# Attention and a gated MLP on one core: scores and P times V by half tiles of queries, with the last scores in the bank of P times V

## The chip, the cores and the metric

One NeuronCore of a Trainium2 chip runs the whole program in one launch. The metric is device microseconds of one execution. The core has a matrix engine (TensorE, PE in the profile, with PEld for its weight loads), three other compute engines (VectorE or DVE, ScalarE or ACT, GpSimd or POOL), and SyncE (SP), which issues the transfers. All of them run their own queue of instructions in order and wait for each other by semaphores. TensorE writes to PSUM, which the kernel uses in banks of 128 partitions by 512 words of 4 bytes; DVE and ACT read it from there.

## The reference

```python
# 8 batches, 8 heads, 576 positions, 64 columns per head
scores = q @ k.T / sqrt(64) + bias            # bias = -slope[h] * |i - j|
mask   = (i - j >= 0) & (i - j < 128)         # a query sees itself and the 127 keys before it
attn   = softmax(where(mask, scores, -1e9))
x      = (attn @ v), heads side by side       # 8 x 576 x 512
h      = relu(x @ w_in)                       # 512 x 1024
u, v   = h[..., :512], h[..., 512:]
v_n    = (v - mean) / sqrt(var + 1e-6)        # over the 512 columns
v_s    = w_spatial @ v_n + b_spatial          # over the 576 positions
out    = (u * v_s) @ w_out                    # 512 x 512
```

All of it is float32. A query of tile t (128 queries, five tiles, the last of 64) needs keys of tiles t-1 and t alone; a half tile of 64 queries needs just 192 keys, its own 64 and the 128 before them.

## The kernel before, in words

The work is 32 pairs of heads, four to a batch, and behind each batch its gated MLP. The first five pairs (batch 0, and the first of batch 1) go another way (`raw_tile`, L418), which the change leaves as it is but for names. The other 27 pairs go through `products` (scores), `scores` and `attention`.

**Scores** (`products`, L504, the matmuls on L514). For each tile t of queries and each head j one float32 product of 64 rows (the head's columns), up to 128 queries and up to 256 keys. The two heads of a pair lie in the upper and the lower 64 rows of the array, and go to different PSUM banks. Tiles 0 and 1 share a bank per head, 2 and 3 the next (tag `s`, four buffers), and tile 4 gets a buffer of the tag `x`. DVE adds bias and mask and takes the minimum (L525), ACT takes exp (L531); later ACT and DVE make from that the two float16 parts of P (L566, L571), and SP transposes them by DMA into `pt` (L577). `prob` and `pq` have one buffer per head.

**P times V** (`attention`, the matmuls on L633). Keys stand in the rows, 64 columns of V in the array's columns, one head in each column half. For each tile of keys (`WINDOWS`) a product over all queries that see it, so each has between 32 and 256 columns; each is made three times (vh with the upper part of P, vh with the lower, vl with the upper), for two heads: 42 products to a pair. They gather in two buffers of the tag `x`, 288 queries in each; ACT (L642) and DVE (L646) take them out into `xt`.

**The gated MLP** is made of units, each with a bank of the tag `m` (two buffers): V units (L698, four of 128 positions and L720 for the last 64, with a layer norm behind each on DVE), U units (L750), S units (over positions, L771) and O units (L797).

**The order** is no one's handwriting. Each op is entered in a `Plan` with the engine, a weight in ns, a due time, and what it reads and writes. `Plan.order` runs a list scheduler over these weights: on each engine the ready op with the least due time goes next, and an op that ACT or DVE can do goes to the one that it reckons is done first. The instructions are then issued in that order, and stay so. A changed weight on TensorE can so move work on every engine. Buffers of a tag go round: the op that takes a buffer waits for the users of the one that had it before. Scores of a pair are entered ahead of P times V of the pair before it (`AHEAD`), so the tag `x` goes to tile 4 of the next pair and P times V of this one in turn.

Of the kernel before, what the change touches and what calls it, by code (L numbers as in the profile page):

```python
# [45 lines left out]
class Plan:  # L46
# [8 lines left out]
    def __init__(self):  # L55
        self.ops, self.tags = [], {}

    def buf(self, pool, tag, bufs, shape, dtype):
        line = self.tags.setdefault(tag, [])
        before = line[-bufs] if len(line) >= bufs else None  # L60
        line.append(Buf(lambda: pool.tile(shape, dtype, tag=tag, name=tag, bufs=bufs), before, line[-1] if line else None))
        return line[-1]
# [76 lines left out]
def attn_gmlp_kernel(ctx, tc, qk, v, w_in, w_spT, b_sp, w_out, outT):  # L139
# [3 lines left out]
    nc = tc.nc  # L143
# [34 lines left out]

    def fixed(shape, dtype, name):
        t = const.tile(shape, dtype, name=name)  # L180
        return Buf(lambda: t)
# [10 lines left out]
    def pe(*cols):  # L192
        return sum(11 + n / 2.4 for n in cols)
# [34 lines left out]
    def constants():  # L228
# [28 lines left out]
        plan.add("DVE", 150, 501, f, [(ident, 0)], [(minus, 0)])  # L257
        for j in range(2):
            def f(j=j):
                nc.vector.memset(stat[j](), 1.0)  # L260
            plan.add("DVE", dve(64), 600, f, (), [(stat[j], x) for x in range(99)])
# [158 lines left out]
    def raw_tile(b, p, t, raw, vr, xt, slot, due):  # L420
# [35 lines left out]
        tp = plan.buf(ps, *(("m", 2) if b == 0 else ("s", 4)), [P, 512], F32)  # L456

        def f():
            for i, (k, w) in enumerate(blocks):
                for j in range(2):  # L460
                    c = (2 * i + j) * m
                    nc.tensor.transpose(tp()[:w, c:c + m], pr[j]()[:, i * P:i * P + w], ident()[:m, :m])
# [4 lines left out]
        if len({w for _, w in blocks}) == 1:  # L467
            e = len(blocks) * 2 * m
            copy(e, lambda: (pf(P, 0, e), tp()[:, :e]), due + 1500, [(tp, 0)], pcols)
        else:  # L470
            for i, (k, w) in enumerate(blocks):
                copy(2 * m, lambda i=i, w=w: (pf(w, 2 * i * m, 2 * (i + 1) * m), tp()[:w, 2 * i * m:2 * (i + 1) * m]), due + 1500,
                     [(tp, 0)], pcols[i::len(blocks)])
# [19 lines left out]
    def clear():  # L493
        for j in range(2):
# [4 lines left out]
    BANKS = (((0, 1), ("s", 4)), ((2, 3), ("s", 4)), ((4,), ("x", 2)))  # L499

    WINDOWS = (((0, 0, 256, 0), (1, 256, 160, 128), (2, 512, 32, 256)),
               ((1, 416, 96, 0), (2, 544, 224, 0), (3, 768, 192, 96), (4, 1024, 64, 224)))

    def products(p, due, st, raw, RAWS, g, banks):  # L504
# [5 lines left out]
        def f():  # L510
            for k, i, t, m, k0, k1 in span:
                for j in range(2):
                    rows = slice(j * D, (j + 1) * D)
                    nc.tensor.matmul(sc[k][j]()[:m, i, :k1 - k0], raw()[rows, 0, t * P:t * P + m], raw()[rows, 1, k0:k1],  # L514
                                     start=True, stop=True)
        plan.add("PE", SWITCH + pe(*[4 * (x[5] - x[4]) for x in span]), due - 5000 + g * 3000, f, RAWS,
# [65 lines left out]
    def attention(p, due, vr, VRS, pts):  # L582
# [5 lines left out]
        def f():  # L588
            nc.scalar.activation(vl(), vr(), AF.Abs, accum_out=am()[:, 0:1])
# [33 lines left out]
        xt = plan.buf(work, "xt", 6, [P, 2 * S + R], F32R)  # L623
        xps = [plan.buf(ps, "x", 2, [P, 512], F32) for _ in range(2)]

        def f():
            for hf, xp in enumerate(xps):
                seen = set()
                for kt, o, n, x0 in WINDOWS[hf]:
                    for l, a in ((vh, 0), (vh, 1), (vl, 0)):  # L630
                        for j in range(2):
                            rhs = pts[j]()[:, a * NB:(a + 1) * NB, :].rearrange("p a b -> p (a b)")
                            nc.tensor.matmul(xp()[j * D:(j + 1) * D, x0:x0 + n], l()[:, kt, j * D:(j + 1) * D], rhs[:, o:o + n],  # L633
                                             start=j not in seen, stop=False, skip_group_check=True)
                            seen.add(j)
        plan.add("PE", SWITCH + pe(*[n for w in WINDOWS for _, _, n, _ in w for _ in range(3)]), due + 5000, f,
                 [(vh, 0), (vl, 0), (pts[0], 0), (pts[1], 0)], [(xp, 0) for xp in xps])
        for hf, xp in enumerate(xps):
            qs = slice(hf * HS, (hf + 1) * HS)

            def f(xp=xp, qs=qs):
                nc.scalar.activation(xt()[:, qs], xp()[:, :HS], AF.Copy, scale=am()[:, 6:7])  # L642
            plan.add("ACT", act(HS, 1), due + 2500 + hf, f, [(xp, 0), (am, 1)], xcols(xt, 0, hf * HS, (hf + 1) * HS))

            def f(xp=xp, qs=qs, hf=hf):
                nc.vector.scalar_tensor_tensor(xt()[:, S + R + hf * HS:S + R + (hf + 1) * HS], xp()[:, :HS], am()[:, 6:7], xt()[:, qs].bitcast(F32),  # L646
                                               ALU.mult, ALU.subtract)
            plan.add("DVE", dve(HS), due + 2600 + hf, f, [(xp, 0), (am, 1)] + xcols(xt, 0, hf * HS, (hf + 1) * HS), xcols(xt, 1, hf * HS, (hf + 1) * HS))
# [243 lines left out]
```

## Time and profile before

| | |
|---|---|
| runs | 635.79, 638.85 and 638.37 us, median 638.37 |
| profiled execution | 636.62 us, span 634.9 us from its first to its last instruction, 1.7 us around it |
| TensorE busy | 605.2 us, 95% of the span, granted clock 0.987 on the mean |
| DVE, ACT, POOL busy | 538.9, 421.0, 29.9 us |

Busy times are unions of the instructions' spans. A matmul is shown from its start to its modelled end, so starts tell more than ends. "x16" counts instructions; a float32 product of L514 shows as two MATMUL rows, with a weight load each. In the chain of work that ended last, a piece is the time from its first start to the next piece's.

### The profile page before, as it was taken

What the parts mean: (1) busy time and instruction counts of PE and PEld (TensorE: products, weight loads), DVE (VectorE), ACT (ScalarE), POOL (GpSimd) and SP (SyncE); (2) the same over time, 40 slices, a digit from 0 to 9 for tenths busy, and PEclk for the clock granted to TensorE, in tenths of its full rate; (3) what the DMA queues carried; (4) which work ended last, traced back from release to release, by engine and by line L of the source; (5) the groups of instructions that cost most, each with busy time, mean ns of one, the idle gap of its engine ahead of it and who ended that gap; (6) DMA issues with size and microseconds to landing.
All of it is one profiled execution on the core that took longest, in us unless ns stands there. A gap on an engine that the chain in (4) does not pass through costs nothing.

```text
span 634.9 us, 14049 instructions
## 1 busy us (share of the span) xinstructions
PE 605.2 (95%) x4956; PEld 526.5 (83%) x4956; DVE 538.9 (85%) x1973; ACT 421.0 (66%) x1300; POOL 29.9 (5%) x53
## 2 busy tenths in 40 slices
PE   4879899799899899999999999999999999999997
PEld 2455588688699888999899988998899888998997
DVE  6999898988979899998899899998998899983532
ACT  4698674897856675966497577876596668753211
POOL 1000010000100001000100001000200010000100
PEclk9997799999999999999999999999999999999999
DMA  8903123698845853587555762696558861651001
GB/s 267 336 21 98 49 67 101 149 190 183 174 78 118 190 136 97 115 176 179 116 128 119 197 147 80 121 201 158 119 115 154 166 125 24 112 126 45 1 23 53
DMA packets 153610, 80.22 MB, mean 126 GB/s; under 512 B 132930, under 2 KB 144194, under 8 KB 153540
## 3 DMA queue, kind: packets, MB, share of 16 engines
q1 hardware_dynamic: 153540, 79.32, 53.6%
q8 instruction: 39, 0.64, 0.4%
q14 instruction: 31, 0.25, 0.1%
HBM read 37.13 MB, written 9.44 MB: 73 GB/s over the span
## 4 chain that ended last, share of the span: by engine, by line
PE 62%; DVE 2%; DMA 2%; ACT 1%; issue 0%; ACTq 0%; DVEq 0%
PE m L771 15%; PE m L750 12%; PE m L797 11%; PE m L698 10%; PE s L514 5%; PE x L633 5%; PE m L720 2%; PE x L514 1%; DMA vl<-vl 1%; DMA out_dram<-o 1%; DVE pq L571 1%; DVE xt L646 0%; ACT prob L531 0%; DVE vl L620 0%; DVE o L271 0%
## 5 line engine op out<-in xcount | busy, mean ns | idle before, releaser
L531 ACT ACTIVATE prob<-prob,stat 128x256 f32<-128x256 f32 (+2 forms) x270 | 125.5, 468 | 44.7 <-DVE stat L525 44.7
L771 PE MATMUL m<-wsp,vn 128*128 128x288 f32 x768 | 121.5, 298 | 2.8 <-DVE o L271 2.8
L771 PEld LDWEIGHTS m<-wsp,vn 128*128 128x128 f32 x768 | 107.2, 188 | 6.3 <-DVE o L271 3.4
L750 PE MATMUL m<-xt,win 128*128 128x288 f32 x768 | 111.4, 298 | 0.3 <-ACT u L275 0.3
L797 PE MATMUL m<-gs,wout 128*128 128x288 f32 x768 | 109.6, 298 | 0.1
L566 ACT ACTIVATE pq<-prob,stat 128x128 f16<-128x128 f32 x270 | 104.5, 469 | 5.6 <-ACT prob L531 2.9
L750 PEld LDWEIGHTS m<-xt,win 128*128 128x128 f32 x768 | 104.0, 188 | 4.6 <-issue 1.7
L797 PEld LDWEIGHTS m<-gs,wout 128*128 128x128 f32 x768 | 103.0, 188 | 4.2 <-issue 2.6
L571 DVE SCALAR_TENSOR_TENSOR pq<-prob,stat,pq 128x128 f16<-128x128 f32 x270 | 105.2, 433 | 1.2 <-ACT pq L566 0.7
L698 PE MATMUL m<-win,xt 128*128 128x512 f32 x384 | 92.8, 396 | 2.0 <-DVE vt L729 1.6
L698 PEld LDWEIGHTS m<-win,xt 128*128 128x128 f32 x384 | 72.7, 191 | 19.1 <-issue 2.3
L525 DVE CUSTOM_DVE_ANT_0 prob<-s,tab 128x256 f32<-128x256 f32 (+2 forms) x222 | 75.2, 377 | 0.9
L514 PE MATMUL s<-qkraw 64*128 64x256 f32 (+2 forms) x444 | 52.2, 370 | 3.7 <-DVE stat L525 3.7
L779 DVE TENSOR_TENSOR u<-m,u 128x288 f32<-128x288 f32 x64 | 28.9, 452 | 30.6 <-PE m L771 30.1
L668 POOL TENSOR_TENSOR st<-st,nhalf 128x1 f32<-128x1 f32 (+1 forms) x40 | 25.9, 647 | 548.4 <-DVE st L664 535.5
L531 ACT ACTIVATION_READ_ACCUMULATOR prob<-prob,stat 128x1 f32 (+1 forms) x270 | 51.2, 190 | 0.0
L514 PEld LDWEIGHTS s<-qkraw 64*128 64x128 f32 (+1 forms) x444 | 37.1, 189 | 12.7 <-issue 4.8
L633 PE MATMUL x<-pt,vh 128*64 128x256 f16 (+6 forms) x756 | 41.7, 229 | 0.0
L275 ACT ACTIVATE vt<-m 128x512 f32<-128x512 f32 x32 | 19.1, 596 | 28.6 <-DVE st L663 18.9
L659 DVE BATCH_NORM_STATS2 st<-vt 128x6 f32<-128x512 f32 (+1 forms) x40 | 27.5, 687 | 9.6 <-ACT vt L275 9.6
L633 PEld LDWEIGHTS <-vh 128*64 128x64 f16 x756 | 31.7, 110 | 4.6 <-issue 4.6
L633 PE MATMUL x<-pt,vl 128*64 128x256 f16 (+6 forms) x378 | 35.3, 228 | 0.0
(131 smaller groups left out, 821.2 us busy)
## 6 DMA issues: line engine op xcount, KB each, us to landing
qkraw<-in_qk_dram SPq DMA_DIRECT2D x28, 576.0 KB, 3.8
out_dram<-o SPq DMA_DIRECT2D x64, 144.0 KB, 2.5
vraw<-in_v_dram SPq DMA_DIRECT2D x28, 320.0 KB, 3.2
vn<-in_w_in_dram SPq DMA_DIRECT2D x6, 512.0 KB, 6.7
pt<-in_w_out_dram SPq DMA_DIRECT2D x4, 512.0 KB, 4.6
gs<-in_w_spT_dram SPq DMA_DIRECT2D x4, 288.0 KB, 5.2
xt<-in_w_in_dram SPq DMA_DIRECT2D x2, 512.0 KB, 6.3
qkraw<-in_qk_dram SPq DMA_DIRECT2D x3, 320.0 KB, 8.7
```

The costliest lines, as they stand in the source:

```text
L514: nc.tensor.matmul(sc[k][j]()[:m, i, :k1 - k0], raw()[rows, 0, t * P:t * P + m], raw()[rows, 1, k0:k1], start=True, stop=True)
L525: nc.vector.tensor_tensor_reduce(pt(), sc()[:m, i, :n], tabs[h]()[:m, c0:c0 + n], -0.125, 3e38, ALU.add, ALU.min, st()[:m, NM, j, t:t + 1])
L531: nc.scalar.activation(pt(), pt(), AF.Exp, bias=st()[:m, NM, j, t:t + 1], scale=-1.0, accum_out=st()[:m, SM, j, t:t + 1])
L566: nc.scalar.activation(pq[j]()[:m, 0, cs], prob[j]()[:m, cs], AF.Copy, scale=st()[:m, RC, j, t:t + 1])
L571: nc.vector.scalar_tensor_tensor(pq[j]()[:m, 1, cs], prob[j]()[:m, cs], st()[:m, RC, j, t:t + 1], pq[j]()[:m, 0, cs], ALU.mult, ALU.subtract)
L633: nc.tensor.matmul(xp()[j * D:(j + 1) * D, x0:x0 + n], l()[:, kt, j * D:(j + 1) * D], rhs[:, o:o + n], start=j not in seen, stop=False, sk ...
L659: nc.vector.bn_stats(st()[:m, 0:6], vt()[:m])
L698: nc.tensor.matmul(pt(), xt[c]()[:, X0[a] + t * P:X0[a] + (t + 1) * P], win()[:, c, w, DH:DF], start=(n == 0), stop=(n == 3 * NC_ - 1))
L750: nc.tensor.matmul(pt()[:, :HS], win()[:, c, w, d * P:(d + 1) * P], xt[c]()[:, X0[a] + hf * HS:X0[a] + (hf + 1) * HS], start=(n == 0), sto ...
L771: nc.tensor.matmul(pt()[:, :HS], l, r, start=(n == 0), stop=(n == len(ops) - 1))
L779: nc.vector.tensor_tensor(u(), pt()[:, :HS], u(), ALU.mult)
L797: nc.tensor.matmul(pt()[:, :HS], wout()[:, d, w, e * P:(e + 1) * P], gs[d]()[:, a, :], start=(n == 0), stop=(n == 3 * ND - 1))
```

## The change

Scores: a tile of queries is cut in halves of 64, and each half is multiplied with its own 192 keys alone (fewer in tile 0). A product now uses 64 rows and 64 columns of the array, a quarter of it: head by rows, half by columns. What a half leaves out of the tile's 256 columns is masked anyway; so that it is a number, the second halves of the `s` banks are set to zero once at the start.

P times V: by halves of 64 queries. One set of products takes 128 rows (a whole tile of keys), the other 64 rows (the half tile at either end of the 192 keys); two of these lie side by side in the upper and lower rows and go to different banks. All have 64 columns: 96 products to a pair. One `x` bank now holds the five first halves of tiles (320 words), the other the four second halves (256). The last 192 words of both banks hold the scores of tile 4 (tag `y`), which so have no buffer in common with P times V any more. The tiles of the tags `s`, `x` and `y` are made once and kept.

```diff
+    plan.kept["s"] = [ps.tile([P, 2, 2 * P], F32, name=f"s{k}") for k in range(4)]
+    plan.kept["x"] = [ps.tile([P, 512], F32, name=f"x{k}") for k in range(2)]
+    plan.kept["y"] = [x[:, 512 - 3 * D:].rearrange("p (a b) -> p a b", a=1) for x in plan.kept["x"]]
...
+        for k in range(4):
+            plan.add("DVE", 340, 100, lambda k=k: nc.vector.memset(plan.kept["s"][k][:, 1, :], 0.0))
...
-    BANKS = (((0, 1), ("s", 4)), ((2, 3), ("s", 4)), ((4,), ("x", 2)))
-
-    WINDOWS = (((0, 0, 256, 0), (1, 256, 160, 128), (2, 512, 32, 256)),
-               ((1, 416, 96, 0), (2, 544, 224, 0), (3, 768, 192, 96), (4, 1024, 64, 224)))
+    BANKS = (((0, 1), ("s", 4)), ((2, 3), ("s", 4)), ((4,), ("y", 2)))
...
             for k, i, t, m, k0, k1 in span:
-                for j in range(2):
-                    rows = slice(j * D, (j + 1) * D)
-                    nc.tensor.matmul(sc[k][j]()[:m, i, :k1 - k0], raw()[rows, 0, t * P:t * P + m], raw()[rows, 1, k0:k1],
-                                     start=True, stop=True)
-        plan.add("PE", SWITCH + pe(*[4 * (x[5] - x[4]) for x in span]), due - 5000 + g * 3000, f, RAWS,
+                for q in range(t * P, t * P + m, D):
+                    for j in range(2):
+                        rows, out = slice(j * D, (j + 1) * D), slice(q - t * P, q - t * P + D)
+                        a, z = max(k0, q - P), q + D
+                        nc.tensor.matmul(sc[k][j]()[out, i, a - k0:z - k0], raw()[rows, 0, q:q + D], raw()[rows, 1, a:z],
+                                         start=True, stop=True, skip_group_check=True)
+        plan.add("PE", SWITCH + pe(*[4 * min(x[5] - x[4], 3 * D) for x in span]), due - 5000 + g * 3000, f, RAWS,
...
+        whole = [w for k in range(NQ - 1) for w in ((k, 1, k, P * 2 * k + D), (k, 0, k + 1, P * (2 * k + 1)))]
+        parts_ = [[(k, 0, k, P * 2 * k, 0)] + [(k, 1, k + 1, P * (2 * k + 1) + D, D)] * (k < NQ - 2) for k in range(NQ)]
...
+            def product(l, a, kt, half, t, o, rows):
+                for j in range(2):
+                    rhs = pts[j]()[:, a * NB:(a + 1) * NB, :].rearrange("p a b -> p (a b)")
+                    nc.tensor.matmul(xps[half]()[j * D:(j + 1) * D, t * D:(t + 1) * D], l()[rows, kt, j * D:(j + 1) * D], rhs[rows, o:o + D],
+                                     start=(half, j) not in seen, stop=False, skip_group_check=True)
+                    seen.add((half, j))
+            for group in parts_:
+                for l, a in ((vh, 0), (vh, 1), (vl, 0)):
+                    for kt, half, t, o, r in group:
+                        product(l, a, kt, half, t, o, slice(r, r + D))
+            for kt, half, t, o in whole:
+                for l, a in ((vh, 0), (vh, 1), (vl, 0)):
+                    product(l, a, kt, half, t, o, slice(0, P))
+        plan.add("PE", SWITCH * 3 // 2 + pe(*[D] * 3 * (len(whole) + len(parts_))), due + 5000, f,
...
```

The weights of both ops change with it, and the scheduler lays everything behind them anew. First place: TensorE, from a V stretch into the next scores, a middle batch of the kernel before (L698 and L720 are V units, L514 scores, L750 U units, L633 P times V).

```order
L797 MATMUL m<-gs,wout 128x288 x24
L698 MATMUL m<-win,xt 128x512 x12
L720 MATMUL m<-win,xt 128x512 x8
L698 MATMUL m<-win,xt 128x512 x36
L514 MATMUL s<-qkraw 128x128 x2
L514 MATMUL s<-qkraw 128x256 x6
L514 MATMUL x<-qkraw 64x192 x2
L750 MATMUL m<-xt,win 128x288 x24
L633 LDWEIGHTS vh
L633 MATMUL x<-pt,vh 64x256
```

Every middle batch has this form: five V units in one piece, then scores. The same place in one of the changed kernel's batches (L826 is O, L727 and L749 are V, L524 scores):

```order
L826 MATMUL m<-gs,wout 128x288 x12
L727 MATMUL m<-win,xt 128x512 x12
L524 MATMUL s_67<-qkraw 64x64
L524 MATMUL s_68<-qkraw 64x64
L524 MATMUL s_67<-qkraw 64x128
L524 MATMUL s_68<-qkraw 64x128
L524 MATMUL s_67<-qkraw 64x192
L524 MATMUL s_68<-qkraw 64x192
```

Scores now stand behind the first V unit. Further on in the same V stretch:

```order
L524 MATMUL x_70<-qkraw 64x192
L524 MATMUL x_71<-qkraw 64x192
L749 MATMUL m<-win,xt 128x512 x8
L727 MATMUL m<-win,xt 128x512 x12
L650 LDWEIGHTS vh
L650 MATMUL x_70<-pt,vh 64x64
L650 LDWEIGHTS vh
L650 MATMUL x_70<-pt,vh 64x64
```

Scores and P times V of a pair were both moved in between V units; in the next batches they stand elsewhere, and the form comes again only after three batches. Second place: TensorE, the end of that P times V, where the 64 columns of every product are seen, and what stands behind it.

```order
L650 LDWEIGHTS vl
L650 MATMUL x_70<-pt,vl 64x64
L650 LDWEIGHTS vl
L650 MATMUL x_70<-pt,vl 64x64
L727 MATMUL m<-win,xt 128x512 x24
L779 MATMUL m<-xt,win 128x288 x60
```

In this batch five U units follow in one piece (L779), where before two, one and two of them stood around P times V and scores.

## Rows read from the trace of the kernel before

**Rows 1.** The page, busy time of each engine.
```profile
PE 605.2 (95%) x4956; PEld 526.5 (83%) x4956; DVE 538.9 (85%) x1973; ACT 421.0 (66%) x1300; POOL 29.9 (5%) x53
```
**Rows 2.** Windows of 100 us: start:end, length, then busy us and instructions per engine.
```profile
100.00:200.00 100.00, 93.72 (x809) 81.30 (x808) 87.80 (x336) 74.10 (x241) 4.30 (x7) 0.98 0.65 144
200.00:300.00 100.00, 98.02 (x887) 89.04 (x887) 90.34 (x339) 69.46 (x227) 3.29 (x5) 1.00 0.65 147
300.00:400.00 100.00, 100.00 (x832) 88.93 (x832) 91.86 (x334) 72.54 (x223) 6.50 (x10) 1.00 0.59 136
```
**Rows 3.** The chain that ended last, one batch: start us, us, what.
```profile
301.05 2.77 PE m L698 x12
...
313.89 1.72 PE s L514 x16
315.61 0.47 PE x L514 x4
316.09 3.39 PE m L750 x24
319.48 1.51 PE x L633 x42
...
322.78 1.72 PE s L514 x16
...
328.34 1.84 PE m L771 x14
...
342.19 1.72 PE s L514 x16
...
360.09 1.72 PE s L514 x16
...
362.28 3.37 PE m L797 x24
...
370.52 0.70 PE m L698 x3
```
**Rows 4.** Timeline of TensorE in one P times V: start us, us, instructions.
```profile
250.47 0.21 PE L633 MATMUL x<-pt,vh 128*64 128x32 f16 x4
...
250.56 0.26 PE L633 MATMUL x<-pt,vh 128*64 128x96 f16 x4
...
251.23 0.23 PE L633 MATMUL x<-pt,vh 128*64 128x64 f16 x4
251.29 0.20 PE L633 MATMUL x<-pt,vl 128*64 128x64 f16 x2
251.42 0.40 PE L750 MATMUL m<-xt,win 128*128 128x288 f32 x1
```
**Rows 5.** Line 514, weight loads: ns least/median/most, first and last start.
```profile
L514 PEld LDWEIGHTS s<-qkraw x444: 129/187/334, 108.8 to 552.9; 64*128 64x128 f32 x144, 64*64 64x64 f32 x4
L514 PEld LDWEIGHTS x<-qkraw x96: 129/130/133, 148.1 to 553.5; 64*64 64x64 f32 x96
```
**Rows 6.** Windows by stretches of the batch of rows 3, columns as in rows 2.
```profile
301.05:313.90 12.85, 12.85 (x59) 10.25 (x57) 11.73 (x35) 7.45 (x15) 2.15 (x3) 1.00 0.63 123
313.90:322.80 8.90, 8.90 (x100) 7.83 (x100) 8.39 (x34) 6.08 (x22) 1.10 (x2) 1.00 0.30 98
322.80:337.00 14.20, 14.20 (x112) 13.34 (x112) 12.96 (x55) 13.74 (x48) 0.00 (x0) 1.00 0.67 129
337.00:346.40 9.40, 9.40 (x104) 8.50 (x104) 8.98 (x34) 5.48 (x19) 0.00 (x0) 1.00 0.64 126
346.40:354.50 8.10, 8.10 (x93) 7.90 (x92) 7.65 (x30) 7.14 (x25) 0.00 (x0) 1.00 0.65 176
354.50:370.50 16.00, 16.00 (x153) 14.93 (x153) 13.90 (x55) 10.33 (x36) 0.00 (x0) 1.00 0.74 182
```
**Rows 7.** Timeline of DVE at the start.
```profile
1.17 0.27 DVE L234 MEMSET u<- 128x256 f32 x1
...
3.32 0.91 DVE L265 SCALAR_TENSOR_TENSOR tab<-u 128x256 bf16<-128x256 f32 x2 [1.78 <-POOL u L239]
```

More of the change, by code (lines that the diff above doesn't have):

```diff
@@ L55, in __init__ @@
     def __init__(self):
-        self.ops, self.tags = [], {}
+        self.ops, self.tags, self.kept = [], {}, {}
     def buf(self, pool, tag, bufs, shape, dtype):
@@ L60, in buf @@
         before = line[-bufs] if len(line) >= bufs else None
-        line.append(Buf(lambda: pool.tile(shape, dtype, tag=tag, name=tag, bufs=bufs), before, line[-1] if line else None))
+        kept = self.kept.get(tag)
+        make = (lambda k=len(line) % bufs: kept[k]) if kept else lambda: pool.tile(shape, dtype, tag=tag, name=tag, bufs=bufs)
+        line.append(Buf(make, before, line[-1] if line else None))
         return line[-1]
@@ L455, in raw_tile @@
                         due + 1000, cols[j] + [(rstat, row)], cols[j])
-        tp = plan.buf(ps, *(("m", 2) if b == 0 else ("s", 4)), [P, 512], F32)
+        tp = plan.buf(ps, *(("m", 2) if b == 0 else ("s", 4)), [P, 2, 2 * P], F32)
+        flat = lambda: tp().rearrange("p a b -> p (a b)")
         def f():
@@ L461, in f @@
                     c = (2 * i + j) * m
[L462 removed]
+                    nc.tensor.transpose(flat()[:w, c:c + m], pr[j]()[:, i * P:i * P + w], ident()[:m, :m])
         plan.add("PE", SWITCH // 2 + pe(*[2 * m] * 2 * len(blocks)), due + 1300, f, cols[0] + cols[1] + [(ident, 0)], [(tp, 0)])
@@ L468, in raw_tile @@
             e = len(blocks) * 2 * m
-            copy(e, lambda: (pf(P, 0, e), tp()[:, :e]), due + 1500, [(tp, 0)], pcols)
+            copy(e, lambda: (pf(P, 0, e), flat()[:, :e]), due + 1500, [(tp, 0)], pcols)
         else:
             for i, (k, w) in enumerate(blocks):
-                copy(2 * m, lambda i=i, w=w: (pf(w, 2 * i * m, 2 * (i + 1) * m), tp()[:w, 2 * i * m:2 * (i + 1) * m]), due + 1500,
+                copy(2 * m, lambda i=i, w=w: (pf(w, 2 * i * m, 2 * (i + 1) * m), flat()[:w, 2 * i * m:2 * (i + 1) * m]), due + 1500,
                      [(tp, 0)], pcols[i::len(blocks)])
@@ L623, in attention @@
         xt = plan.buf(work, "xt", 6, [P, 2 * S + R], F32R)
+        swap = len(plan.tags["x"]) % 2
         xps = [plan.buf(ps, "x", 2, [P, 512], F32) for _ in range(2)]
+        both, xps = xps, xps[::-1] if swap else xps
+        whole = [w for k in range(NQ - 1) for w in ((k, 1, k, P * 2 * k + D), (k, 0, k + 1, P * (2 * k + 1)))]
+        parts_ = [[(k, 0, k, P * 2 * k, 0)] + [(k, 1, k + 1, P * (2 * k + 1) + D, D)] * (k < NQ - 2) for k in range(NQ)]
         def f():
[L627 to L648, printed above, removed]
+            seen = set()
@@ new lines, in f @@
+            for kt, half, t, o in whole:
+                for l, a in ((vh, 0), (vh, 1), (vl, 0)):
+                    product(l, a, kt, half, t, o, slice(0, P))
+        plan.add("PE", SWITCH * 3 // 2 + pe(*[D] * 3 * (len(whole) + len(parts_))), due + 5000, f,
+                 [(vh, 0), (vl, 0), (pts[0], 0), (pts[1], 0)], [(xp, 0) for xp in both])
+        for half, xp in enumerate(xps):
+            k = NQ - half
+            n = k * D
+            hi = lambda half=half, k=k: xt()[:, 0:k * P].rearrange("p (k a) -> p k a", a=P)[:, :, half * D:(half + 1) * D]
+            c0 = S + R - D * (1 - half)
+            lo = lambda c0=c0, k=k: xt()[:, c0:c0 + k * P].rearrange("p (k a) -> p k a", a=P)[:, :, D:P]
+            src = lambda xp=xp, n=n: xp()[:, :n].rearrange("p (k a) -> p k a", a=D)
+            xh, xl = ([c for t in range(k) for c in xcols(xt, a, t * P + half * D, t * P + (half + 1) * D)] for a in range(2))
+            def f(hi=hi, src=src):
+                nc.scalar.activation(hi(), src(), AF.Copy, scale=am()[:, 6:7])
+            plan.add("ACT", act(n, 1), due + 2500 + half, f, [(xp, 0), (am, 1)], xh)
+            def f(hi=hi, lo=lo, src=src):
+                nc.vector.scalar_tensor_tensor(lo(), src(), am()[:, 6:7], hi().bitcast(F32), ALU.mult, ALU.subtract)
+            plan.add("DVE", dve(n), due + 2600 + half, f, [(xp, 0), (am, 1)] + xh, xl)
```

## The prediction

> **What bounds the kernel now.** First the page: TensorE is busy 605.2 of 634.9 us, DVE 538.9, ACT 421.0 [rows 1]. That share is a mean, so the windows come next: between 100 and 200 us TensorE is idle for 6.28 us of 100, between 200 and 300 for 1.98, between 300 and 400 for nothing, and there DVE is busy 91.86 [rows 2]. Third, the chain that ended last: over a whole batch, from 301.05 to 370.52, 69.47 us, it is TensorE alone, unit behind unit [rows 3]. Scores of a pair take 1.72 + 0.47 us there, P times V 1.51, four of each to a batch. So TensorE sets the time in the middle of the program, with DVE close behind; a microsecond taken from TensorE counts until DVE or ACT ends a wait first.
>
> **Scores.** A product's time is its columns, in two passes (x16 rows for eight products). The row of 0.47 us holds 192 columns, so 384 column passes, a first weight load and the change to the next unit; that of 1.72 us holds 128 + 3 x 256 = 896 columns, 1792 passes, a longer first load and the same change [rows 3]. The longer load (128 columns instead of 64) is 187 - 130 = 57 ns more [rows 5]. The difference gives a pass: (1.72 - 0.47 - 0.057) / 1408 = 0.847 ns; what is left of 0.47 is 0.145 us for load and change. After the change a tile's four products (two heads, two halves) can run side by side in the four quarters of the array, and the tile takes as long as its longer half: 128 + 3 x 192 + 192 = 896 columns, 1792 passes, 1.518 us, and as tile 4 has the same form as the others there is one load and one change: 1.518 + 0.145 = 1.66 us for 2.19. That is 0.53 less, 14.3 us over 27 pairs. The bound on the other side is that the halves run one behind the other: 64 + 128 + 7 x 192 = 1536 columns, 3072 passes, 2.75 us, 0.56 more. Nothing before shows four at once. But the two row halves share the 0.47 us, and the two column halves of P times V share a step (next), so I take 1.66.
>
> **P times V.** Two heads side by side make a step. A step of 64 columns takes 0.03 us (two steps from 251.23 to 251.29), and one of 32 columns no less (three from 250.47 to 250.56); from the last step's end, 251.32, to the next unit 0.10 us pass [rows 4]. The changed form has 24 steps with 128 rows and 15 with 64 rows (in nine of these, four products side by side), all of 64 columns: 39 x 0.03 = 1.17 us, 0.10 for the change from half rows to whole rows in the middle, 0.10 at the end, one step for the first load: 1.40 instead of 1.51, 0.11 less, 3.0 us over 27 pairs. If the nine fours take two steps each, it is 1.67, 0.16 more. There are 96 products instead of 42, and as many weight loads. I take 1.40, since the nearest row, 64 columns, shows no further cost.
>
> Together TensorE has 0.64 us less per pair, **17.3 us in all**.
>
> **What stands beside it.** The taking out of `xt` has as many columns and instructions as before (320 + 256 for 2 x 288). The minimum and exp still work on whole tiles, so DVE and ACT lose nothing. I cost that at zero; it lies beside TensorE's units, and where DVE or ACT is full, the floor below takes it in. P times V now needs both `x` banks at its first steps, before the second only at its fourth window, some 0.6 us later; with `y` apart the banks are free long before, so zero, at most 0.6 us a pair if not. Scores of tile 4 no longer wait for the taking out of the pair before; in the batch of [rows 3] no such wait is seen, so zero too. Four memsets of 256 columns at 0.27 us stand on DVE ahead of the constants, 1.1 us; DVE is idle there for 1.78 us, waiting for POOL [rows 7]. Zero, 1.1 if that cover is gone.
>
> **The floor.** Where DVE or ACT is nearly as busy as TensorE, only the difference can be gained. By stretches of one batch [rows 6], with 0.53 for each scores and 0.11 for each P times V: 313.90 to 322.80 would become 8.26, but DVE has 8.39, gain 0.51; 322.80 to 337.00 would become 13.67, but ACT has 13.74, gain 0.46; 337.00 to 346.40 gives 0.42 (DVE 8.98 of 9.40); 346.40 to 354.50 0.11; the last 0.64. That is 2.14 of 2.56, and so 14.5 of 17.3 us.
>
> **The order.** The scheduler lays the work anew. Adding the durations of [rows 3] along both orders, with the new ones for scores and P times V, consecutive scores start 23.0, 8.7, 19.5 and 17.6 us apart in every middle batch before (the chain shows 8.9, 19.4 and 17.9 [rows 3]). Changed, they start 12.1, 9.6, 27.8, 13.8, 9.6, 7.2, 12.3, 40.3, 12.1, 9.6, 17.6, 27.1 us apart, and the form repeats after three batches only. Scores and P times V also fall between V units, whose stretch before had none and yet holds DVE for 11.73 of 12.85 us [rows 6]. In-order queues on DVE and ACT turn such bunches into waits: units behind late scores find no free `m` bank. The price has two bounds in the trace: 0 per 100 us where the order is even, 6.28 where it isn't yet (the scores of 100 to 200 us start 8.6, 4.0, 17.3, 10.2 us apart by the same sum) [rows 2]. The change is uneven throughout, but without the first batches' loads; I take the middle, 3.14 per 100 us, from 200 to 600 us: 12.6 us, ends 0 and 25.1.
>
> **Sum.** -14.5 + 12.6 = -1.9 us. The profiled execution is 636.62, which is 1.75 below the median shown; against it that is 634.7, against the median of 638.37 it is **636.5 us**, no change that can be told: a measurement of this kernel tells about 0.5% (3.2 us) from none.
>
> **Rivals.**
> - *The even flow stays.* Buffers absorb the bunches, and only the floor holds: 638.4 - 14.5 = 623.9. For it: TensorE is idle for nothing between 300 and 400 us, so there is slack behind it. Against it: DVE's 91.86 of 100 would become 95 and more.
> - *The uneven order costs its full price,* 25.1 us: 638.4 + 10.6 = 649. Place: U and O units that wait for a bank which ACT or DVE has not emptied. It decides from 3.6 us of idle TensorE per 100 us on (14.5 over four hundreds), and makes the kernel slower by what is above that.
> - *Each small product takes a step of its own,* whether its neighbours are in other quarters or not: 96 x 0.03 + 0.23 = 3.11 us, 1.60 more per pair, 43 us; less 14.3 is 29, so 667. From 2.04 us for P times V on TensorE has lost. Against it: two heads share a step of 0.03 us now, but only for six products in a row. The Trainium skill (TensorE: Matmul & The Clock Gate, "Wait — 56ns, not 53.3ns?") has a rule of this kind: matmuls never start less than about 25 ns apart, however few their columns; by that, 96 products would be an estimated 2.4 us. The rows don't bear it out for neighbours in different halves, whose starts share one step.
> - *The change doesn't do what it says:* the halves of a tile run one behind the other. Scores 2.75, P times V 1.40: 0.45 more per pair, 12 us, 650 before any cost of the order. Against it: each kind of neighbour, by rows and by columns, runs together now.
>
> **How the numbers follow.** Forecast 0.53, of which 0.08 lies over 0.5% faster; even flow 0.25; full price of the order 0.12; own steps 0.06; halves in a row 0.04. So faster 0.33, same 0.45, slower 0.22. The range leaves out the last two cases, the lowest of the even flow and the upper half of the full price: 625 to 646. The likeliest case's own range is 632 to 641.
>
> **What would show it.** Right: in the profile after, P times V of 96 products takes about 1.4 us from its first start to the next unit's and scores 1.66; TensorE's busy time falls by some 17 us, yet its idle time grows by nearly as much, with waits of U, O and V units for ACT and DVE in the middle windows; DVE's busy time stays within 3 us. Wrong: TensorE still full between 300 and 400 us (the even flow), P times V over 2 us, or scores over 2.2.

## The result, and the profile after

The changed kernel takes **642.96 us** in the median of five runs (641.63 to 644.11), against 638.37 (635.79 to 638.85) before on the same chip: a ratio of 1.0096, with an interval of 1.0074 to 1.0118. It is slower by 1%, where the prediction had 636.5 us and no difference that can be told. The profiled execution took 643.79 us, with a span of 641.8.

Lines have moved: scores are L524 now (L514 before), their minimum L535 (L525), P times V L650 (L633), the taking out of `x` into `xt` L672 on ACT and L676 on DVE (L642, L646); V, U, S and O units are L727, L779, L800 and L826.

The page of the changed kernel, busy time of each engine:

```profile
PE 601.1 (94%) x6846; PEld 523.4 (82%) x6846; DVE 534.1 (83%) x1956; ACT 434.1 (68%) x1321; POOL 30.1 (5%) x53
```

TensorE's busy time falls by only 4.1 us from [rows 1], and its idle time grows from 29.7 (634.9 - 605.2) to 40.7 us. Windows of the changed kernel, columns as in [rows 2]:

```profile
100.00:200.00 100.00, 92.10 (x1163) 81.35 (x1163) 89.42 (x341) 75.83 (x239) 4.72 (x7) 0.93 0.70 147
200.00:300.00 100.00, 96.49 (x1245) 87.00 (x1244) 85.96 (x331) 73.20 (x233) 3.29 (x5) 1.00 0.63 140
300.00:400.00 100.00, 95.94 (x1234) 85.31 (x1233) 90.21 (x319) 70.83 (x216) 6.54 (x10) 0.98 0.60 133
```

TensorE, which was full between 300 and 400 us, now waits for 4 us there, and DVE is no busier than before. The next two fences are the busy time of single lines over the whole span (the union of a line's matmuls, then of its weight loads). Before, with scores, P times V and O in that order:

```profile
sum 642.00, PE 63.51 PEld 41.79; mean PE 63.51 PEld 41.79
...
sum 642.00, PE 42.55 PEld 39.55; mean PE 42.55 PEld 39.55
...
sum 642.00, PE 109.63 PEld 102.99; mean PE 109.63 PEld 102.99
```

After, the same three:

```profile
sum 642.00, PE 48.12 PEld 35.99; mean PE 48.12 PEld 35.99
...
sum 642.00, PE 42.11 PEld 37.68; mean PE 42.11 PEld 37.68
...
sum 642.00, PE 114.47 PEld 106.42; mean PE 114.47 PEld 106.42
```

The two kinds of product do cost TensorE 15.8 us less: 15.4 in the scores, 0.4 in P times V. But O units, which did not change, cost 4.8 us more. Of these, 3.6 lie between 100 and 200 us, where 96 of their matmuls stand in either kernel. The windows hold O units alone: first before, then the changed kernel, then a stretch of the changed kernel at the lower of the clock's two levels (0.50 in the profile, 1.2 GHz).

```profile
100.00:200.00 100.00, 14.39 (x96) 12.97 (x96) 0.98 0.65 144
...
100.00:200.00 100.00, 18.01 (x96) 16.21 (x96) 0.93 0.70 147
...
122.20:132.40 10.20, 3.74 (x15) 3.74 (x16) 0.50 1.01 211
```

So most of the 4.8 us is the granted clock of this one execution. TensorE had been idle for 3.4 us, waiting for DVE, around the point where the clock fell; it rose again while an O unit ran. Over all stretches at the lower level, before (47.7 to 54.5, 71.6 to 78.4, 126.3 to 129.7 us) and then after (43.6 to 53.8, 71.0 to 77.8, 122.2 to 132.4, 152.9 to 156.3, 323.5 to 326.9):

```profile
sum 17.00, PE 15.51 PEld 9.41 DVE 14.67 ACT 12.44 POOL 0.00; mean PE 5.17 PEld 3.14 DVE 4.89 ACT 4.15 POOL 0.00
...
sum 34.00, PE 30.14 PEld 21.80 DVE 30.27 ACT 26.01 POOL 1.26; mean PE 6.03 PEld 4.36 DVE 6.05 ACT 5.20 POOL 0.25
```

TensorE was busy at that level for 14.6 us more than before. Half of that, an estimate of 7 us, is busy time that full clock would have spared; it hides some 7 of the 11.7 us (15.8 - 4.1) that the busy time does not show as saved. The rest is not accounted for.

TensorE's waits in front of whole units are the other sign. O and U units of the changed kernel, then U and O units of before; the number behind the second bar, with what ended it, is the idle time of TensorE in front of them:

```profile
L826 PE MATMUL m<-gs,wout 128*128 128x288 f32 x768 | 114.5, 305 | 5.6 <-DVE u L808 2.2 <-ACT o L281 1.9 <-DVE gs L814 0.9
L779 PE MATMUL m<-xt,win 128*128 128x288 f32 x768 | 112.5, 300 | 5.0 <-ACT vt L285 3.6 <-ACT u L285 1.2
...
L750 PE MATMUL m<-xt,win 128*128 128x288 f32 x768 | 111.4, 298 | 0.3 <-ACT u L275 0.3
L797 PE MATMUL m<-gs,wout 128*128 128x288 f32 x768 | 109.6, 298 | 0.1
```

Together 10.6 us, where before they waited 0.4. These are waits for ACT and DVE, most of them, by what ended them, for a bank that one of the two had not emptied yet. Another wait, on ACT, is seen in the chain that ended last (start us, us, what), at a place that has no like in [rows 3]:

```profile
497.75 1.47 PE x L650 x96
499.21 1.35 PE s L524 x28
500.57 0.26 PE x L524 x4
500.83 0.52 ACT xt L672
501.35 0.02 issue
501.37 0.94 DVE xt L676 x2
```

P times V ends at 499.21. ACT takes `x` out only 1.6 us later, when the scores that stand right behind it are done. Not all of that is a wait for them; the timeline of ACT has other work (L576) until 500.28, and 0.53 us of idle time:

```profile
497.63 2.65 ACT L576 ACTIVATE pq<-prob,stat 128x128 f16<-128x128 f32 x7
500.81 0.90 ACT L672 ACTIVATE xt<-x,am 128x320 fp32r<-128x320 f32 x2 [0.53 <-PE x L524]
```

Those scores' last products are tile 4's (`PE x L524`): they go to `y`, the free columns of the same two banks. In the waits of the changed kernel (engine, line, waited for: us in total, times, longest) this is a row of its own, the second:

```profile
DVE xt L676 <- ACT xt L672: 14.5, 9, 7.3
...
ACT xt L672 <- PE x L524: 9.8, 8, 2.6
...
DVE prob L535 <- PE x L524: 7.3, 4, 1.8
```

Of the 14.5 us in the first row only 6.3 stand behind the eight waits of the second. One wait of 7.3 us is near the end of the program (585 us), where no scores are left, and one of 1.0 at 349 us follows none of the eight. The kernel before has no row like the second; its rows that answer to the first and the third are:

```profile
DVE prob L525 <- PE x L514: 5.4, 9, 0.9
DVE xt L646 <- ACT xt L642: 3.9, 3, 3.4
```

In TensorE's list of the changed kernel scores follow P times V directly for 8 of 27 pairs; in the list of before for none.

### The profile page after: what moved, and what is told of

The parts are those of the page before. It is cut to its first block, busy times and chain, and to the rows that moved or that the text cites. A ratio compares the mean times of both kernels' runs of the same rounds, so it can differ in the third digit from the quotient of the medians.

```text
span 641.8 us, 17856 instructions
## 1 busy us (share of the span) xinstructions
PE 601.1 (94%) x6846; PEld 523.4 (82%) x6846; DVE 534.1 (83%) x1956; ACT 434.1 (68%) x1321; POOL 30.1 (5%) x53
## 3 DMA queue, kind: packets, MB, share of 16 engines
q1 hardware_dynamic: 153540, 79.32, 53.8%
## 5 line engine op out<-in xcount | busy, mean ns | idle before, releaser
L800 PE MATMUL m<-wsp,vn 128*128 128x288 f32 x768 | 121.8, 297 | 2.1 <-DVE u L808 1.4
L826 PE MATMUL m<-gs,wout 128*128 128x288 f32 x768 | 114.5, 305 | 5.6 <-DVE u L808 2.2
L826 PEld LDWEIGHTS m<-gs,wout 128*128 128x128 f32 x768 | 106.4, 194 | 13.2 <-DVE u L808 3.4
L779 PE MATMUL m<-xt,win 128*128 128x288 f32 x768 | 112.5, 300 | 5.0 <-ACT vt L285 3.6
L779 PEld LDWEIGHTS m<-xt,win 128*128 128x128 f32 x768 | 105.5, 190 | 9.9 <-ACT vt L285 5.7
L800 PEld LDWEIGHTS m<-wsp,vn 128*128 128x128 f32 x768 | 107.4, 188 | 5.3 <-DVE u L808 1.9
L576 ACT ACTIVATE pq<-prob,stat 128x128 f16<-128x128 f32 x270 | 105.2, 466 | 5.4 <-ACT prob L541 2.2
L727 PE MATMUL m<-win,xt 128*128 128x512 f32 x384 | 94.1, 397 | 2.7 <-DVE vt L286 1.2
L727 PEld LDWEIGHTS m<-win,xt 128*128 128x128 f32 x384 | 71.1, 189 | 22.0 <-ACT vt L285 2.1
L535 DVE CUSTOM_DVE_ANT_0 prob<-s,tab 128x256 f32<-128x256 f32 (+2 forms) x222 | 74.3, 380 | 0.7
L285 ACT ACTIVATE u<-m 128x288 f32<-128x288 f32 x48 | 19.5, 406 | 42.3 <-PE m L779 42.0
L524 PE MATMUL s<-qkraw 64*64 64x192 f32 (+2 forms) x876 | 43.0, 318 | 4.8 <-DVE stat L535 4.8
L650 PEld LDWEIGHTS <-vh 64*64 64x64 f16 (+1 forms) x1728 | 36.0, 110 | 8.1 <-issue 6.8
L650 PE MATMUL x<-pt,vh 64*64 64x64 f16 (+1 forms) x1728 | 41.3, 196 | 1.0 <-DMA pt<-pq 1.0
L524 PEld LDWEIGHTS s<-qkraw 64*64 64x64 f32 x876 | 31.4, 136 | 10.1 <-DVE stat L535 6.0
L650 PE MATMUL x<-pt,vl 64*64 64x64 f16 (+1 forms) x864 | 38.9, 194 | 0.0
L676 DVE SCALAR_TENSOR_TENSOR xt<-x,am,xt 128x320 fp32r<-128x320 f32 (+1 forms) x54 | 25.3, 511 | 14.6 <-ACT xt L672 14.5
```

Of the source, the lines that this page charges most:

```text
L524: nc.tensor.matmul(sc[k][j]()[out, i, a - k0:z - k0], raw()[rows, 0, q:q + D], raw()[rows, 1, a:z], start=True, stop=True, skip_group_chec ...
L535: nc.vector.tensor_tensor_reduce(pt(), sc()[:m, i, :n], tabs[h]()[:m, c0:c0 + n], -0.125, 3e38, ALU.add, ALU.min, st()[:m, NM, j, t:t + 1])
L576: nc.scalar.activation(pq[j]()[:m, 0, cs], prob[j]()[:m, cs], AF.Copy, scale=st()[:m, RC, j, t:t + 1])
L650: nc.tensor.matmul(xps[half]()[j * D:(j + 1) * D, t * D:(t + 1) * D], l()[rows, kt, j * D:(j + 1) * D], rhs[rows, o:o + D], start=(half, j ...
L676: nc.vector.scalar_tensor_tensor(lo(), src(), am()[:, 6:7], hi().bitcast(F32), ALU.mult, ALU.subtract)
L727: nc.tensor.matmul(pt(), xt[c]()[:, X0[a] + t * P:X0[a] + (t + 1) * P], win()[:, c, w, DH:DF], start=(n == 0), stop=(n == 3 * NC_ - 1))
```

## Experiments

**Theory 1:** the products are cheaper, and the new order gives it back. **Theory 2:** a part of that is the wait at the bank which `x` and `y` share. **Theory 3**, formed after the first four runs: not the new weights but the buffers of their own for tile 4 made the order uneven, and the wait too. The rival throughout: the small products themselves cost elsewhere. Ratios are against runs of the kernel before on the same chip, whose median was 636.0 to 636.1 us there. The changed kernel at its ratio of 1.0096 is 642.2 us on that scale; with its own median, 642.96, each difference to it would be 0.8 us larger.

### New products, old order

```diff
-    BANKS = (((0, 1), ("s", 4)), ((2, 3), ("s", 4)), ((4,), ("y", 2)))
+    BANKS = (((0, 1), ("s", 4)), ((2, 3), ("s", 4)), ((4,), ("x", 2)))
...
-        plan.add("PE", SWITCH + pe(*[4 * min(x[5] - x[4], 3 * D) for x in span]), due - 5000 + g * 3000, f, RAWS,
+        plan.add("PE", SWITCH + pe(*[4 * (x[5] - x[4]) for x in span]), due - 5000 + g * 3000, f, RAWS,
```

P times V and the taking out of `x` have their old weights too, and the four memsets are issued ahead of the list. TensorE's units then stand exactly as before.

> The half-tile products of the change, with TensorE's units in the order of the kernel before, tile 4 in the banks of x in turn as there. Theory 1 (the products are cheaper and the new order gives it back): TensorE spends 15.8 us less on the two kinds of product in the trace of the changed kernel (63.51 to 48.12 for the scores, 42.55 to 42.11 for P times V); where DVE or ACT is nearly as full, a part of it is lost, as the floor of the prediction had it, so 624 to 629 us. Rival (the small products themselves cost elsewhere: twice the matmuls, more code to load, a lower granted clock): 636 us or more, whatever the order.

Measured: 631.75 us, ratio 0.9928 (0.9905 to 0.9952). Faster than both kernels, so the small products are not the cost, and theory 1 has its sign. But 4.4 us is much less than the 7 to 12 expected; the runs with less work on DVE come back to that.

### Old products, changed order

The scores and P times V of the kernel before, put into the changed kernel's list, weights and buffers:

```diff
-                for q in range(t * P, t * P + m, D):
-                    for j in range(2):
-                        rows, out = slice(j * D, (j + 1) * D), slice(q - t * P, q - t * P + D)
...
+                for j in range(2):
+                    rows = slice(j * D, (j + 1) * D)
+                    nc.tensor.matmul(sc[k][j]()[:m, i, :k1 - k0], raw()[rows, 0, t * P:t * P + m], raw()[rows, 1, k0:k1],
+                                     start=True, stop=True)
```

> The whole-tile products of the kernel before, in exactly the order of the changed kernel on every engine, tile 4 in the bank of x as there. Theory 1 (the order costs): clearly slower than before, 645 to 655 us: the changed kernel's 643 us, plus that part of the 15.8 us of product time which TensorE does not spend waiting anyhow. Rival (the order costs nothing, the products do): 638 us, as before.

Measured: 655.51 us, ratio 1.0299 (1.0268 to 1.0330), just above the upper end. With nothing gained on the products, the changed list and its buffers cost 19.4 us. The half-tile products win 13.3 of them back (655.5 to 642.2).

### Tile 4 first

```diff
-            for k, i, t, m, k0, k1 in span:
+            for k, i, t, m, k0, k1 in sorted(span, key=lambda x: x[2] != NQ - 1):
```

> The changed kernel with one edit: in the last unit of scores of a pair, tile 4 (whose products go to the free columns of the two x banks) is computed first and not last. Nothing else moves on any engine. In the changed kernel ACT waits 8 times for these products before it may take x out, 9.8 us in all, and DVE 14.5 us behind it. Theory 2 (the shared bank is a part of the cost): that wait falls from about 1.2 us to a few tenths each time, and the time falls by 2 to 5 us, to 638 to 641. If the order alone does it, these waits only stand where others would: 642 to 644.

Measured: 636.79 us, ratio 1.0009 (0.9992 to 1.0027). That is 5.4 us less than the changed kernel, a little more than expected, without a move on any engine. The waits of this kernel:

```profile
DVE xt L676 <- ACT xt L672: 9.3, 4, 7.3
...
ACT xt L672 <- PE x L524: 3.1, 3, 1.5
...
DVE prob L535 <- PE x L524: 2.8, 4, 0.8
```

All three rows shrink, the second from 9.8 to 3.1 us. Theory 2 fits. But the edit shortens two waits at once: the taking out of `x` behind tile 4 (6.7 us less on ACT), and the minimum of tile 4, which DVE has first in its queue (4.5 us less). The second is no matter of the bank, as the kernel before has it too (5.4 us). They were not parted, so how much of the 5.4 us is the shared bank is not shown.

### Banks in turn, new weights

```diff
-    BANKS = (((0, 1), ("s", 4)), ((2, 3), ("s", 4)), ((4,), ("y", 2)))
+    BANKS = (((0, 1), ("s", 4)), ((2, 3), ("s", 4)), ((4,), ("x", 2)))
```

> The changed kernel with tile 4 back in the two x banks in turn (so no bank is shared at one time), with the new weights of the units, so that the list is laid out anew: TensorE's order differs from the changed kernel's in 159 of 372 places, and is as uneven as that. Theory 1: the shared bank's waits go, the unevenness stays: 636 to 641 us. If the shared bank is all of it: as with the old order, 624 to 629. If neither, 643 us.

Measured: 633.31 us, ratio 0.9956 (0.9939 to 0.9972). Below what theory 1 gave it, and the expectation was wrong in its premise: this list is not uneven. TensorE's units differ from those of before in 29 of 372 places, where the changed kernel's differ in 159. The scores in its timeline (start us, us, instructions):

```profile
382.74 1.42 PE L522 MATMUL s<-qkraw 64*64 64x64 f32 x32
390.96 1.42 PE L522 MATMUL s<-qkraw 64*64 64x64 f32 x32
410.80 1.42 PE L522 MATMUL s<-qkraw 64*64 64x64 f32 x32
428.20 1.42 PE L522 MATMUL s<-qkraw 64*64 64x64 f32 x32
451.05 1.42 PE L522 MATMUL s<-qkraw 64*64 64x64 f32 x32
```

They are 8.2, 19.8, 17.4 and 22.9 us apart, the form of [rows 3]. So the new weights alone did not bend the list. What was left was the other edit, tile 4's own buffers, and theory 3.

### Only tile 4's own buffers

The kernel before, with `kept` added to the scheduler as in the change, and:

```diff
+    plan.kept["x"] = [ps.tile([P, 512], F32, name=f"x{k}") for k in range(2)]
+    plan.kept["y"] = [x[:, 512 - 3 * D:].rearrange("p (a b) -> p a b", a=1) for x in plan.kept["x"]]
...
-    BANKS = (((0, 1), ("s", 4)), ((2, 3), ("s", 4)), ((4,), ("x", 2)))
+    BANKS = (((0, 1), ("s", 4)), ((2, 3), ("s", 4)), ((4,), ("y", 2)))
```

> The kernel before with one edit: tile 4's scores go to the free columns of the two x banks, as buffers of their own (y), and no longer to the x banks in turn. Products, weights and everything else as before; the scheduler lays its list anew (TensorE's differs in 144 of 372 places from before). Theory 3 (this edit alone makes the order uneven and sets up the waits at the shared bank): 645 to 655 us, as the old products in the changed order (655.5). Rival (the new weights of the shorter products made the order uneven): 635 to 638 us.

Measured: 658.46 us, ratio 1.0341 (1.0318 to 1.0365): 22.4 us slower by this edit alone, more than expected. Its scores in the timeline:

```profile
374.10 1.79 PE L519 MATMUL s<-qkraw 64*128 64x128 f32 x16
384.80 1.79 PE L519 MATMUL s<-qkraw 64*128 64x128 f32 x16
405.32 1.79 PE L519 MATMUL s<-qkraw 64*128 64x128 f32 x16
433.13 1.79 PE L519 MATMUL s<-qkraw 64*128 64x128 f32 x16
448.50 1.79 PE L519 MATMUL s<-qkraw 64*128 64x128 f32 x16
```

10.7, 20.5, 27.8 and 15.4 us apart, and for 6 pairs directly behind P times V. Its waits hold the row of the changed kernel (L647 takes `x` out, L519 are the scores):

```profile
ACT xt L647 <- PE x L519: 8.8, 6, 1.7
```

Theory 3 holds: this edit alone gives an uneven list and the wait, and the 22.4 us hold both. The code says why: a buffer's next user waits, in the scheduler's own reckoning, for every user of the buffer two places before it. With tile 4 in turn with `x`, scores cannot be listed before the P times V ahead of them has been taken out. In the trace before no matmul waits for that (weight loads do, 1.0 us in all), and it kept the two apart.

### The changed order, twice more

The old products in the changed list, with tile 4 first:

```diff
-            for k, i, t, m, k0, k1 in span:
+            for k, i, t, m, k0, k1 in sorted(span, key=lambda x: x[2] != NQ - 1):
```

> The whole-tile products in the changed kernel's order (the second experiment, 655.5 us) with tile 4 computed first in its unit. If the wait at the shared bank grows with the unit that stands in front of it (1.72 us of other tiles there instead of 1.35), this gives back 6 to 8 us: 647 to 650 us. If the unevenness alone costs the 19 us: 653 to 656.

Measured: 645.03 us, ratio 1.0128 (1.0107 to 1.0149). 10.5 us come back, more than expected and twice what the short products gave back. So with whole tiles the 19.4 us are 10.5 that go with tile 4's place in its unit, and 8.9 that stay with the changed list.

The changed kernel with tile 4 first, and the old weights:

```diff
-        plan.add("PE", SWITCH + pe(*[4 * min(x[5] - x[4], 3 * D) for x in span]), due - 5000 + g * 3000, f, RAWS,
+        plan.add("PE", SWITCH + pe(*[4 * (x[5] - x[4]) for x in span]), due - 5000 + g * 3000, f, RAWS,
```

P times V has its old weight here as well.

> The changed kernel with tile 4 first and the weights that the two kinds of product had before. Tile 4 keeps its own buffers, so by theory 3 the order stays uneven (112 of 372 places of TensorE differ from the changed kernel's, 140 from the kernel before) and the time near that of the changed kernel with tile 4 first: 635 to 639 us. If the weights made the order uneven: 631 to 633, as with the banks in turn.

Measured: 647.11 us, ratio 1.0163 (1.0139 to 1.0187). Not the even order's time, as theory 3 says, but 10.3 us above the same kernel with the new weights, which no theory had. With the bank ring cut, the same change of two weights moves the time by 10 us. With the ring in place it moved it by 1.6 (631.75 and 633.31, where the weights of the taking out of `x` changed too). So without the ring the weights do bend the list; why this one is so much slower stays open.

### Each product alone

The first experiment with one of its two parts taken back to the kernel before, so that TensorE's order is again that of before. Scores alone, in diff against the first experiment (P times V and the taking out of `x` go back the same way):

```diff
-            for group in parts_:
...
+            for hf, xp in enumerate(xps):
+                seen = set()
+                for kt, o, n, x0 in WINDOWS[hf]:
```

> Only the scores by half tiles; P times V, the taking out of x and the order of every engine as in the kernel before. If the gain of the half tiles under the old order (631.75 us against 636.1) is that of the scores, as TensorE's times say (15.4 us of the 15.8), then 630 to 632 us. If P times V by halves has a cost of its own (its parts need both x banks taken out before the first V and U unit can run), this is faster than with both: 626 to 630 us. If P times V brought it: 635 to 637.

Measured: 634.70 us, ratio 0.9982 (0.9964 to 1.0001). P times V alone (the scores go back as in the second experiment):

```diff
-                for q in range(t * P, t * P + m, D):
...
+                for j in range(2):
+                    rows = slice(j * D, (j + 1) * D)
```

> Only P times V by half tiles; the scores by whole tiles, TensorE's units in the order before. By TensorE's times (42.55 to 42.11 us over 27 pairs) it is worth 0.4 us: 635 to 637. If both banks being needed before the first V and U unit costs something: 638 us or more. The prediction had 3 us for it: 633.

Measured: 636.69 us, ratio 1.0004 (0.9988 to 1.0021), as expected. Neither gives much alone. The scores miss their expectation: 1.3 us for 15.4 us of TensorE, where both together give 4.4. The lists of DVE and ACT in the run with the scores alone are those of before. In the run with P times V alone they are those of the first experiment, which differ a little, by neighbours that change places. So the scores by halves are worth 1.3 us under the first pair of lists and 4.9 (636.69 - 631.75) under the second. Whether the lists make that difference, or P times V by halves, stays open.

### Less work on DVE

In the kernel before and in the first experiment:

```diff
-            nc.vector.bn_stats(st()[:m, 0:6], vt()[:m])
+            nc.vector.bn_stats(st()[:m, 0:6], vt()[:m, :64])
```

> The kernel before, with the statistics of the layer norm taken over the first 64 of 512 columns (the computation is changed so): DVE has some 0.55 us less for each of 40 instructions, 20 us in all, and nothing else changes. Theory: TensorE is the limit in the middle of the kernel before, DVE nowhere but in the first batches, so little is gained: 631 to 635 us. If DVE is the limit already, 10 us or more: 626.

Measured: 634.43 us, ratio 0.9980 (0.9966 to 0.9994), as expected.

> Both products by half tiles in the old order of TensorE (the first experiment of this study), with the same statistics over 64 columns. Theory: under the old order only 4.4 of TensorE's 15.8 us show, since DVE's order and load set the pace from there on; with 20 us less on DVE the rest comes out, 10 to 14 us below the kernel before with the same relief: 620 to 625 us. If something else eats it (the clock, the order alone), the distance to that kernel stays 4 to 5 us.

Measured: 624.13 us, ratio 0.9819 (0.9799 to 0.9839), as expected. The instruction fell from 687 to 221 ns, 18.7 us over 40. The kernel before gains 1.6 us from that, the half-tile products under its order 7.6: the distance between them grows from 4.4 to 10.3 us. Windows from 300 to 400 us, the first experiment without the relief:

```profile
300.00:400.00 100.00, 97.08 (x1200) 87.50 (x1199) 91.65 (x337) 72.83 (x224) 6.57 (x10) 1.00 0.61 137
```

And with it:

```profile
300.00:400.00 100.00, 100.00 (x1271) 90.88 (x1271) 89.94 (x351) 75.66 (x237) 6.58 (x10) 1.00 0.63 139
```

TensorE is full again there. Where DVE's work held it up is seen at the U units, first without the relief and then with it:

```profile
L779 PE MATMUL m<-xt,win 128*128 128x288 f32 x768 | 111.3, 298 | 4.1 <-DVE u L282 3.6 <-ACT u L281 0.5
...
L779 PE MATMUL m<-xt,win 128*128 128x288 f32 x768 | 111.0, 298 | 0.6 <-ACT u L281 0.6
```

The 3.6 us in which TensorE waited for DVE to empty the bank of a U unit are gone. So under the old order DVE keeps a part of what was missing, 5.9 (10.3 - 4.4) of 11.4 us (15.8 - 4.4), though it is busy for no more than 92 of 100. The other 5.5 did not come back with this relief. The same relief in the changed kernel with tile 4 first:

> The changed kernel with tile 4 first (636.8 us), with the statistics of the layer norm over 64 of 512 columns. Under the old order this relief of DVE gave 7.7 us (631.75 to 624.13). Theory: what the uneven order still costs, 5 us, is DVE's queue being late in bunches, so the relief gives more here, 10 to 12 us: 624 to 627. If the unevenness costs through the banks of m and ACT instead: 7 us or less, 629 to 632.

Measured: 626.95 us, ratio 0.9852 (0.9827 to 0.9876), 9.8 us less than without, just short of the 10 to 12 expected. What the uneven order still costs is 2.8 us with the relief (626.95 - 624.13) and 5.0 without (636.79 - 631.75). But 2.2 us between the two is no more than what the intervals of the four ratios leave open (1.1 to 1.6 us to either side each), so that DVE's queue is a part of it is a hint and not shown.

## Why the prediction was wrong

Medians on one scale, the changed kernel by its ratio:

| | order and banks of before | tile 4 apart, changed order | the same, tile 4 first |
|---|---|---|---|
| whole-tile products | 636.1 | 655.5 | 645.0 |
| half-tile products | 631.75 | 642.2 | 636.8 |

The change is 4.4 us of gain down the first column and 10.5 of loss along the lower row: 5.4 that go with tile 4's place and 5.0 that stay with the changed list. The sum of the prediction was 14.5 and 12.6. So the gain turned the sign: it was 10.1 us too large, the loss only 2.1. With 14.5 of gain the measured loss would have left the kernel 4.0 us faster. The parts do not simply add: along the upper row and down the middle column it is 19.4 of loss and 13.3 of gain. The prediction took its gain from stretches in the old order, so the first column is what tests it.

**The products: right.** Scores were to take 1.66 us for 2.19. They take 1.61 in the chain above (1.35 + 0.26), and all of them 15.4 us less, against 14.3. Four products side by side is what happens. P times V was to take 1.40 for 1.51, and takes 1.47. Its steps, from the timeline of the changed kernel:

```profile
444.07 0.26 PE L650 MATMUL x<-pt,vh 64*64 64x64 f16 x8
...
444.53 0.20 PE L650 MATMUL x<-pt,vl 64*64 64x64 f16 x2
444.66 0.25 PE L650 MATMUL x<-pt,vh 128*64 128x64 f16 x4
...
445.41 0.20 PE L650 MATMUL x<-pt,vl 128*64 128x64 f16 x2
```

From the first row to the second are 14 steps of half rows, 0.033 us each; from the third to the last 23 steps of whole rows, 0.033 each; between them the 0.10 of the prediction beyond a step. It had read 0.03 from [rows 4], and 39 times 0.003 us, 0.12, is as much as the saving that it looked for; 0.04 of it came.

**A failed step, a term put at nothing: "Scores of tile 4 no longer wait for the taking out of the pair before; in the batch of [rows 3] no such wait is seen, so zero too."** The wait cost TensorE nothing in that batch, true. But it was also what the scheduler kept scores and P times V apart by, and without it the list became what it is. Alone, this edit costs 22.4 us. The prediction did cost the new list, in another term, but not as this edit's. Its neighbour failed with it: "with `y` apart the banks are free long before, so zero, at most 0.6 us a pair if not". That looked at P times V waiting for its banks. The wait that came is the other one: the taking out of `x` waits for scores that write to `y`, 9.8 us on ACT and 6.3 on DVE behind it. `y` had its own columns, but not its own bank. The Trainium skill (PSUM — Partial Sum Buffer, "PSUM bank collisions raise a hardware error") says that two engines must be kept apart on one bank and 32 partitions even where their columns are disjoint. The trace agrees so far as the program has that wait; no run here let both in at once.

**The failed step that turned the sign: the floor.** "That is 2.14 of 2.56, and so 14.5 of 17.3 us." In the old order 4.4 came out. The floor let DVE fill each stretch to the brim. It does not. Over 200 to 600 us, before:

```profile
200.00:600.00 400.00, 397.48 (x3432) 359.50 (x3432) 352.07 (x1282) 271.35 (x848) 19.11 (x30) 1.00 0.58 127
```

And the first experiment:

```profile
200.00:600.00 400.00, 391.31 (x4982) 358.44 (x4982) 351.00 (x1284) 271.01 (x848) 19.24 (x30) 1.00 0.58 128
```

DVE stays at 88%, and the time that TensorE saves turns into 6.2 us more of waiting. DVE also stands idle in waits for other engines (29.7 us in the first experiment for S units' results alone), and its queue is in order, so it can be late for a bank of TensorE's at 88%; that this is how it happens is argued. Shown is that with 18.7 us less work on DVE the gain is 10.3 us, and that TensorE's 3.6 us of waiting for DVE at the U units go with it. The other 5.5 of 15.8 us stay open.

**The order: the size near, the reason half right.** The price was taken at 12.6 us, the middle of 0 and 25.1, a guess between two bounds that came near by luck. Measured, it is 10.5, but half of that goes with tile 4's place in its unit, whose waits were costed at zero. The other half was to come from units that find no free bank; such waits are there, 10.6 us in front of U and O units for 0.4 before, and with tile 4 first 8.2 (4.3 and 3.9). That they are the 5.0 us was not shown. The prediction gave the unevenness no cause. The part on the change names the new weights; the weights alone, with the banks in turn, leave the list nearly as even as it was.

**The profile after.** "TensorE's busy time falls by some 17 us, yet its idle time grows by nearly as much": 4.1 and 11.0. The direction was right; some 7 us of what the 4.1 lacks are the lower clock of the profiled execution (above). "DVE's busy time stays within 3 us": it fell by 4.8 and ACT's rose by 13.1, since the new list gave more of the work that either can do to ACT.

**The rivals.** The even flow (623.9) was not kept; where the first experiment keeps it, it gives 631.75. The uneven order at full price (649) was on the right side: slower, by 1% instead of 1.7%. Products with a step of their own and halves in a row both fell. For the first of these the Trainium skill (TensorE: Matmul & The Clock Gate, "Wait — 56ns, not 53.3ns?") was weighed. By its 25 ns an estimated 2.4 us for 96 products would follow; measured are 1.47 us for all of them, so the rule does not hold between products in different halves or quarters of the array.

The granted clock was 0.93 from 100 to 200 us, against 0.98 in [rows 2], with the lower level from 122.2 to 132.4 us and from 152.9 to 156.3. In the same window it was 0.98 in the first experiment. But the changed kernel's executions with a mean clock of 0.983 took 641.6 to 643.0 us, so the clock is no more than a small part of the loss.

## What to carry to other kernels

Where a scheduler lays the list, every dependency that an edit removes is an edit of the list. Price it by laying the list anew with that edit alone, not by the wait that it shows in the trace. Two results in disjoint columns of one bank were one buffer here for those who read them; if they must share, let the one whose reader is waiting be clear of the other's writer, or write the sharer first. And a saving on the busiest engine is worth only what the next engine's pace leaves of it, and that pace is not its busy share: with DVE at 88%, 11.4 of 15.8 us were lost here, and 5.9 of them came back with less work on DVE. Before a busy time is read as a cost, look at the granted clock of its stretch. The first experiment, half-tile products with the banks in turn as before, is the version to keep: 0.7% faster than the kernel before and 1.7% faster than the change.

## What the hardware showed that was not expected

Four float16 products of 64 by 64 in the four quarters of the array share one step of 0.033 us, as two do. A step of 64 columns took the same here for 64 rows and for 128, for two products and for four.

The taking out of `x` costs the same from blocks of 64 columns as from one piece: 504 ns on DVE and 494 on ACT (medians over blocks of 320 and of 256 columns), against 504 and 489 for 288 columns before.
